# Strided heads of batch 3 brought into the staggered scheme, with their loads moved forward: sparse attention followed by a Mish MLP on one core

## The chip, the cores and the metric

The kernel runs on one core of one Trainium2 chip. The metric is the device time in microseconds of one execution. Before the change it is 306.9 us, the median of three runs (306.23 to 308.34). The profile comes from an execution with a span of 306.6 us on the device, in which TensorE was granted its full clock.

## The reference

Attention over 8 batches, 8 heads, 576 positions and head size 64. Heads 0 to 3 ("local") see the 32 positions up to their own; heads 4 to 7 ("strided") see those earlier positions that are equal to theirs modulo 32. The attention's output, as 4608 tokens by 512, goes through two matrix products with the activation `h * tanh(softplus(h))` (Mish) between them.

```python
scores = scale * np.matmul(q, k.transpose(0, 1, 3, 2))
rel = pos[:, None] - pos[None, :]
mask_local = (rel >= 0) & (rel < stride)                       # stride = 32
mask_strided = (rel >= 0) & (pos[None, :] % stride == pos[:, None] % stride)
masks = np.stack([mask_local if h < H // 2 else mask_strided for h in range(H)], axis=0)
scores = np.where(masks[None, :, :, :], scores, -1000000000.0)
# ... softmax over the last axis ...
attn_out = np.matmul(attn, v)                                  # (8, 8, 576, 64)
x = attn_out.transpose(0, 2, 1, 3).reshape(B * S, H * D)       # (4608, 512)
h = x @ w_in                                                   # (4608, 2048)
sp = np.where(h > 20.0, h, np.log1p(np.exp(np.minimum(h, 20.0))))
out = (h * np.tanh(sp)) @ w_out                                # (4608, 512)
```

## The kernel before

The MLP is done in nine blocks of 512 tokens, t = 0 to 8. In each block `mlp1` is the first product (64 matmuls of 128x128 by 512 columns, then Mish on ScalarE) and `mlp2` the second (also 64). The attention of batch t + 1 is woven into block t, in small pieces between groups of matmuls: list entry i of `at` runs after group i of the second product, entry i of `a1` after group i of the first.

There are two forms for a batch in the middle of the run. In `attn_steps` everything for a batch stands in the second product of one block. In the staggered form, the strided scores of the next batch (kind "n") are made one block ahead, in the second product of the block before; `str_steps` then multiplies them with v in the first product, and `loc_steps` does the local heads in the second. The staggered form also transposes the attention's output on VectorE (`xt_str`, `xt_loc`) instead of TensorE (`xt`).

```python
    def load_qk_str(b):                        # software queue, f32 -> bf16
        for dst, src in ((ks, k), (qs, q)):
            nc.gpsimd.dma_start(dst[b % 2][0:PN], src[b, 4:8].rearrange("h (p j) d -> p h (j d)", j=CS))

    def load_qk_loc(b):                        # SyncE's queue, f32
        for dst, src in ((kl32, k), (ql32, q)):
            nc.sync.dma_start(...)             # [cut]

    # the space of vs32, seen as two bf16 halves
    vsd = vs32[0:PN].rearrange("p h j d -> p (h j d)").bitcast(BF16)
    vsd = [vsd[:, 2048 * i:2048 * i + 2048] for i in range(2)]

    def load_v_str01(b):                       # software queue, f32 -> bf16
        dst = vsd[b % 2].rearrange("p (h x) -> p h x", h=4)
        ...                                    # [cut: batch 0]
            nc.gpsimd.dma_start(dst, v[b, 4:8].rearrange("h (p j) d -> p h (j d)", j=CS))

    def load_v_str(b):                         # SyncE's queue, f32
        nc.sync.dma_start(vs32[0:PN], v[b, 4:8].rearrange("h (p j) d -> p h j d", j=CS))

    def str_by_dma(b):                         # transposed strided k, then q
        for src, dst in ((ks, kTs), (qs, qTs)):
            nc.sync.dma_start_transpose(sT(dst, b)[...], src[b % 2][0:SU]...)   # [cut]

    def str_steps(b):
        a = Attn(b)
        V = lambda i: (lambda: a.pv("s", i))
        return [[], [V(0)], [V(1)], [V(2)], [V(3)], [V(4)], [V(5)], [V(6)], [V(7), a.xt_str]]

    def loc_steps(b, x, y):
        # [cut: Q makes scores and their exponential, M masks on VectorE, V multiplies with v]
        n2 = (("n", 2),) if more else ()
        N = [lambda i=i: a.mask("n", i, nc.gpsimd) for i in range(3)]
        return [
            [],
            [Q(x, ("l", 0)), Q(None, ("l", 2), *n2), Q(y, ("l", 1)), M("l", 0), M("l", 2)],
            [], [],
            [V(0), V(1), M("l", 1)],
            ([Q(x, ("n", 0)), Q(y, ("n", 1))] + N) * more + [a.xt_str_copy, V(5)],
            [V(2)], [V(3)],
            [V(4), lambda: a.xt_loc(0, NW)],
            [], [], [], [], [], [], [],
        ]

    def attn_steps(b, x, y, z=None):           # [cut: its other steps, X transposes on TensorE]
        r = [
            [],
            [Q(x, s0), Q(y, s1), M(*s0), M(*s1)],
            [],
            [V("s", 0), V("s", 1)],
            [Q(x, *sl2), Q(y, l0), V("s", 2)],
            ...
            [X("s", 0), V("l", 2)],
            [X("s", 1), V("l", 3)],
            [V("l", 4), X("l", 0)],
            [X("l", 1)], [],
        ]
        if z is not None:                      # the next batch's strided scores
            r[12].append(Q(x, ("n", 0)))
            r[13].append(Q(z, ("n", 1)))
            r[15] += [Q(x, ("n", 2)), M("n", 0), M("n", 1), M("n", 2)]
        return r
```

Before block 0 the loads of batch 2 are issued, and the loop over blocks issues the later ones:

```python
        load_qk_str(2)
        ...                                    # local q, k of batch 2
        load_v_str01(2)
        load_v_loc_h(2)

        def next_loads():                      # step 1 of block 0's second product
            load_qk_str(3)
            copy_v_str01(2, Po, 0, CS)
            rows_v_loc01(2, 0, 6, Po)

        for t in range(NBLK):
            ...
                if t <= 2:
                    at = attn_steps(t + 1, x, y, z if t == 2 else None)
                elif t + 1 < B:
                    a1 = str_steps(t + 1)
                    at = loc_steps(t + 1, x, y)
                if t == 1:
                    at[9].append(lambda: str_by_dma(3))
                ...
                if t + 2 < B:
                    at[9].append(lambda: loc_by_dma(t + 2))
                if 1 < t < B - 3:
                    at[9].append(lambda: str_by_dma(t + 3))
            ...                                # the first product
            if t > 0 and t + 2 < B:
                cast_qk_loc(t + 2, Po, Po)
                if 1 < t < B - 3:
                    load_qk_str(t + 3)
                if t < 3:
                    cast_v(t + 2, Po, Po)
                else:
                    at[5].append(lambda: cast_v(t + 2, Po, Po))
            if t == 1:
                load_qk_str(4)
            ...                                # the second product
            if t + 3 < B:
                load_qk_loc(t + 3)
                if t == 1:
                    str_by_dma(4)
                load_v(t + 3)
```

Of the kernel before, what the change touches and what calls it, by code (L numbers as in the profile page):

```python
# [40 lines left out]
def kernel(ctx, tc, q, k, v, moe_w_in, moe_w_out, out):  # L41
# [115 lines left out]
    def load_v_str(b):  # L157
        nc.sync.dma_start(vs32[0:PN], v[b, 4:8].rearrange("h (p j) d -> p h j d", j=CS))

    def load_v_loc(b):  # L160
# [2 lines left out]
            vl32[32:128].rearrange("p h w d -> p (h w) d"),  # L163
            v[b, 0:4].rearrange("h (w p) d -> p (h w) d", p=WQ),
        )

    def load_v(b):
        load_v_str(b)
        load_v_loc(b)

    def load_w_in(f0, f1):
        nc.gpsimd.dma_start(  # L172
# [120 lines left out]
    class Attn:  # L293
# [64 lines left out]
        def pv_mm(self, kind, i, po):  # L358
            for h in range(4):
                if kind == "l":  # L360
                    n, rhs = 128, vl[self.b % 2][:, i, h, :]
                    part, u = AT["l"][i, h // 2]
                    pt, c0 = P_l[part][:, h % 2], WQ * u
                else:
                    n, rhs = PN, vs[self.b % 2][0:PN, h, i, :]
                    part, u = AT["n" if self.b > 3 else "s"][i // 2, h]
                    pt, c0 = P_s[part][:, i % 2], PN * u
                nc.tensor.matmul(  # L368
                    po[:, h, :], lhsT=pt[0:n, c0:c0 + 128], rhs=rhs,
                    start=True, stop=True,  # L370
                )
# [250 lines left out]
    with tc.manual_schedule():  # L622
        Po, Dv, Sc = nc.gpsimd, nc.vector, nc.scalar
        Sc.preload_act_table(AF.Exp)
        Sc.dma_start(consts[:], consts_h.ap())
        lq0 = g_pool.tile([128, 16, 512], BF16, tag="gT", name="lq0")
        lq0 = lq0[:].rearrange("p a b -> p (a b)")[0:PL]
        kl0, ql0 = [lq0[:, 1536 * i:1536 * i + 1536].rearrange("p (h x) -> p h x", h=4) for i in range(2)]
        load_str01(ks[0], k, 0)
        load_str01(qs[0], q, 0)  # L630
        load_v_str01(0)
        load_qk_loc01(0, kl0, ql0)
        kl0, ql0 = [x.rearrange("p h (j d) -> p h j d", d=D) for x in (kl0, ql0)]
        Dv.memset(kTs[1][:, 0:640], 0.0)
        Dv.memset(kTs[1][:, 640:], 0.0)
        Dv.memset(vl[0][:, :, :, D:D + 1], 1.0)
        Dv.memset(vl[0][0:32, 0], 0.0)
        load_v_loc01(0, 0, 3)
        load_w_in(0, 256)
        load_v_loc01(0, 3, 6)  # L640
        load_w_in(256, 512)
        load_w_in(512, 1024)
        Dv.memset(vs[0][:, :, :, D:D + 1], 1.0)
        Dv.memset(kTs[0][:, 0:16 * SU].rearrange("p (u n) -> p u n", n=SU)[:, :, PN:], 0.0)
        Dv.memset(kTs[0][:, 16 * SU:], 0.0)
        for p, n in zip(P_s, (6, 6, 4)):
            Dv.memset(p[:, :, n * PN:], 0.0)
        Dv.memset(kTl[:, :, 0:32], 0.0)
        for p, n in zip(P_l, (5, 5, 2)):
            Dv.memset(p[:, :, n * WQ:], 0.0)  # L650
        Dv.memset(vs[1][:, :, :, D:D + 1], 1.0)
        Dv.memset(vl[1][:, :, :, D:D + 1], 1.0)
        Dv.memset(vl[1][0:32, 0], 0.0)
        for x in (ks, qs):
            for h in (0, 2):
                Sc.copy(
                    x[1][64:SU, h:h + 2, :].rearrange("p h x -> p (h x)").bitcast(F32),
                    kTs[1][64:SU, 0:1024].bitcast(F32),
                )

        a = Attn(0)
        fill_acc(2, 11)
        for hp in range(2):
            t_step(0, "k", hp, Sc if hp else Dv)
        a.bias("s", 0, 0)
        fill_acc(2, 4)
        for hp in range(2):
            t_step(0, "q", hp, Sc if hp else Dv)
        a.bias("s", 1, 1)
        fill_acc(2, 1)  # L670
        a.bias("s", 2, 2)
        for i in range(3):
            a.qk([("s", i)], i)
        copy_v_str01(0, Dv, 0, 4)
        copy_v_str01(0, Dv, 4, 8)
        fill(tile_t("fill"), 2)
        a.pv2("s", 0, 0)
        t_step_loc0(kl0, kTl[:, 0, 32:32 + S], 0, Dv)
        t_step_loc0(kl0, kTl[:, 1, 32:32 + S], 1, Sc)
        a.pv2("s", 2, 1)  # L680
        a.pv2("s", 4, 2)
        fill_acc(0, 1)
        t_step_loc0(ql0, qTl[:, 0, :], 0, Sc)
        t_step_loc0(ql0, qTl[:, 1, :], 1, Sc)
        a.pv2("s", 6, 0)
        a.bias("l", 0, 1)
        a.bias("l", 1, 2)
        a.qk([("l", 0)], 1)
        a.qk([("l", 1)], 2)
        rows_v_loc01(0, 0, 3, Po)  # L690
        load_w_in(1024, 1536)
        load_w_in(1536, 2048)
        rows_v_loc01(0, 3, 6, Po)
        load_qk_str(1)
        load_w_out(0, 1)
        load_v_str01(1)
        load_qk_loc01(1, rows(kl[1]), rows(ql[1]))
        load_w_out(1, 3)
        load_v_loc_h(1)
        load_w_out(3, 4)  # L700
        a.bias("l", 2, 0)
        a.qk([("l", 2)], 0)
        a.xt("s", 0, Dv)
        a.xt("s", 1)
        Sc.preload_act_table(AF.Mish)
        a.pv2("l", 0, 1)
        a.pv2("l", 2, 0)
        a.pv2("l", 4, 1)
        accs = (2, 0, 1)
        gT, g1 = mlp1(0, accs)  # L710
        g1.pop(0)()
        a.xt("l", 0)
        g1.pop(0)()
        a.xt("l", 1)
        Dv.memset(vl32[0:32], 0.0)
        for x in (ks, qs):
            Dv.memset(x[0][64:SU], 0.0)
        load_qk_str(2)
        rows_v_loc01(1, 0, 6, Po)
        for dst, src in ((kl, k), (ql, q)):  # L720
            to = by_tile(dst[0])
            for h in range(4):
                nc.gpsimd.dma_start(
                    to[:, h // 2, :, h % 2, :], src[2, h].rearrange("(i p) d -> p i d", p=PL)
                )
        load_v_str01(2)
        load_v_loc_h(2)

        def next_loads():
            load_qk_str(3)  # L730
            copy_v_str01(2, Po, 0, CS)
            rows_v_loc01(2, 0, 6, Po)

        for t in range(NBLK):
            x, y, z = accs
            if t > 0:
                gT, g1 = mlp1(t, accs)
            ts, at, a1 = [], [], []
            if t == 0:
                ts, at = t_steps1(), attn_steps(1, y, y)  # L740
                at[0] += [lambda: Sc.preload_act_table(AF.Exp)]
                at[1] += [lambda: copy_v_str01(1, nc.vector, 0, CS), next_loads]
                at[2] += ts[4:6]
                at[3] += ts[6:8]
                at[9] += [lambda: str_by_dma(2), lambda: loc_by_dma(2)]
                out_accs, accs = (z, x), (y, z, x)
            else:
                if t <= 2:
                    at = attn_steps(t + 1, x, y, z if t == 2 else None)
                elif t + 1 < B:  # L750
                    a1 = str_steps(t + 1)
                    at = loc_steps(t + 1, x, y)
                if t == 1:
                    at[9].append(lambda: str_by_dma(3))
                if t == 2:
                    Dv.memset(x_s[64:96], 0.0)
                if t + 2 < B:
# [3 lines that stand above are left out]
                out_accs, accs = (z, y), (z, x, y)  # L761
            for i, g in enumerate(g1):
                g()
                if i < len(a1):
                    for s in a1[i]:
                        s()
                if t == 0:
                    for n in {6: (0, 1), 7: (2, 3)}.get(i, ()):
                        ts[n]()
            if t > 0 and t + 2 < B:  # L770
                cast_qk_loc(t + 2, Po, Po)
                if 1 < t < B - 3:
                    load_qk_str(t + 3)
                if t < 3:
                    cast_v(t + 2, Po, Po)
                else:
                    at[5].append(lambda: cast_v(t + 2, Po, Po))
            if t == 1:
                load_qk_str(4)
            if t == NBLK - 1:  # L780
                mlp2_last(t, gT, (z, y, x))
                break
            for i, g in enumerate(mlp2(t, gT, out_accs, fc_major=(t == 0))):
                g()
                if i < len(at):
                    for s in at[i]:
                        s()
            if t + 3 < B:
                load_qk_loc(t + 3)
                if t == 1:  # L790
                    str_by_dma(4)
                load_v(t + 3)


# [28 lines left out]
```

## Time and profile before

| | |
|---|---|
| median of 3 runs | 306.9 us |
| span of the profiled execution | 306.6 us |
| VectorE, ScalarE, GpSimd busy | 51%, 60%, 34% of the span |
| TensorE's granted clock | 1.00 |
| mean DMA rate | 136 GB/s |
| read from and written to HBM | 36.82 MB and 9.44 MB |

A row of slices cuts the span into 40 equal parts; a digit is the busy share of one in tenths, 9 being 90% or more. A line of the order in time gives start and length in microseconds, the engine (SPq is SyncE's DMA queue), the line of the kernel, the operation and what it writes and reads; x is the number of instructions merged into it. A queue row gives packets, megabytes and the time its packets took as a share of 16 engines' span.

Names: `psh` is the accumulator of the first product and `pso` that of the second, `ps` holds scores, `po` is attention times v, `trx` the transposes of the attention's output on TensorE. `ks`, `qs`, `vs` are the strided k, q, v; `kl`, `ql`, `vl` the local ones; `kTs`, `qTs`, `kTl`, `qTl` the transposed ones.

### The profile page before, as it was taken

Reading aid. Unit: us, or ns where it says so; the run is one execution under the profiler, and the core shown is the slowest. Engines: PE = TensorE matmul, PEld = TensorE weight load, DVE = VectorE, ACT = ScalarE, POOL = GpSimd, SP = SyncE. Lnnn points to the kernel's source line nnn. Section 1 sums busy time; section 2 is a strip of 40 time slices with the busy share of each in tenths; the row PEclk is TensorE's granted clock in tenths of the full one; section 3 lists DMA queues with packets and bytes.
Section 4 is the critical chain, followed back from the end, with each engine's and each line's share of the span. In section 5 each row is a group of like instructions: output and inputs, shape, how many; then the busy total and the mean of one; then the engine's idle time right before and its main releaser. Section 6 shows DMA issues by size and latency. Waiting matters only on the chain.

```text
span 306.6 us, 5875 instructions
## 1 busy us (share of the span) xinstructions
PE 297.2 (97%) x2431; PEld 154.4 (50%) x2431; DVE 156.8 (51%) x375; ACT 182.9 (60%) x196; POOL 104.0 (34%) x120
## 2 busy tenths in 40 slices
PE   8889999999999999999999999999999999999995
PEld 3544555544554445444578654445444544444444
DVE  3572358201850086579877888787879850000000
ACT  5576553767446763767866786687668746216501
POOL 8592326741246025502980297029600000000000
PEclk9999999999999999999999999999999999999999
DMA  7999999999999999999969996997430120011011
GB/s 112 168 145 201 204 168 145 151 119 186 212 210 134 209 147 209 200 197 193 168 152 179 196 170 147 167 193 125 126 90 0 46 92 0 2 68 68 0 71 68
DMA packets 97558, 41.66 MB, mean 136 GB/s; under 512 B 79612, under 2 KB 91612, under 8 KB 97532
## 3 DMA queue, kind: packets, MB, share of 16 engines
q1 hardware_dynamic: 71564, 28.58, 52.6%
q0 software_dynamic: 25680, 12.46, 35.8%
q8 instruction: 19, 0.31, 0.4%
q10 hardware_dynamic: 288, 0.25, 0.3%
q14 instruction: 7, 0.06, 0.1%
HBM read 36.82 MB, written 9.44 MB: 151 GB/s over the span
## 4 chain that ended last, share of the span: by engine, by line
PE 80%; DMA 11%; DVE 4%; POOL 2%; issue 1%; ACT 0%; POOLq 0%
PE psh L562 36%; PE pso L585 33%; DMA w_out<-in_moe_w_out_dram 5%; PE pso L612 5%; PE po L368 4%; DMA w_in<-in_moe_w_in_dram 3%; DMA lq<-in_q_dram 3%; PE ps L330 3%; DVE x_s L380 1%; DVE Pl L352 1%; DVE x_l L380 1%; DVE rden L379 1%; PE trx L407 1%; POOL w_in L172 0%; POOL ks L110 0%
## 5 line engine op out<-in xcount | busy, mean ns | idle before, releaser
L562 PE MATMUL psh<-xT,w_in 128*128 128x512 bf16 (+1 forms) x640 | 130.6, 358 | 1.0 <-ACT xT L185 0.7
L585 PE MATMUL pso<-w_out,gT 128*128 128x512 bf16 x512 | 121.7, 379 | 0.2 <-DMA w_out<-in_moe_w_out_dram 0.2
L568 ACT ACTIVATE gT<-psh 128x1024 bf16<-128x1024 f32 x72 | 72.4, 1023 | 47.7 <-PE psh L562 47.7
L562 PEld LDWEIGHTS <-w_in 128*128 128x128 bf16 x640 | 60.1, 98 | 56.6 <-issue 1.4
L585 PEld LDWEIGHTS <-gT 128*128 128x128 bf16 x512 | 45.5, 98 | 46.2 <-issue 0.2
L442 DVE STREAM_TRANSPOSE xs_t<-x_s 32x512 bf16<-32x512 bf16 x48 | 33.7, 702 | 0.9
L592 ACT COPY osb<-pso 128x1024 f32<-128x1024 f32 x16 | 17.6, 1099 | 24.6 <-PE pso L585 14.0
L379 DVE RECIPROCAL rden<-po 72x4 f32<-72x4 f32 (+1 forms) x98 | 17.3, 177 | 28.2 <-PE po L368 27.9
L187 POOL CAST kl<-kl 96x768 bf16<-96x768 f32 x10 | 8.5, 876 | 62.3 <-DMA kl<-in_k_dram 53.0
L352 DVE TENSOR_TENSOR Ps<-Ps,consts_sb 72x864 bf16<-72x864 bf16 (+3 forms) x12 | 8.1, 683 | 38.9 <-ACT Ps L344 38.9
L433 DVE STREAM_TRANSPOSE xT<-x_l 32x384 bf16<-32x384 bf16 x48 | 27.3, 569 | 0.7
L187 DVE COPY osb<-pso 128x512 f32<-128x512 f32 (+1 forms) x2 | 1.1, 558 | 51.3 <-PE pso L612 51.3
L380 DVE TENSOR_TENSOR x_s<-po,rden 72x256 bf16<-72x256 f32 x56 | 23.6, 421 | 1.9
L344 ACT ACTIVATE Ps<-ps 72x864 bf16<-72x864 f32 (+3 forms) x21 | 17.4, 860 | 10.7 <-PE ps L330 10.6
L449 ACT COPY xT<-xs_t 128x576 bf16<-128x576 bf16 x8 | 21.4, 2938 | 0.0
L368 PEld LDWEIGHTS <-Ps 72*128 72x128 bf16 x256 | 14.9, 98 | 11.5 <-DVE Ps L352 0.8
L344 ACT ACTIVATE Pl<-ps 128x960 bf16<-128x960 f32 (+1 forms) x20 | 17.1, 875 | 3.7 <-PE ps L330 3.6
L380 DVE TENSOR_TENSOR x_l<-po,rden 96x256 bf16<-96x256 f32 x42 | 17.7, 421 | 1.4
L185 ACT COPY xT<-trx 128x576 bf16<-128x576 bf16 x15 | 9.5, 640 | 14.3 <-PE trx L417 11.7
L368 PE MATMUL po<-vs,Ps 72*128 72x65 bf16 x256 | 17.3, 194 | 0.1
L187 POOL CAST vl<-vl 128x768 bf16<-128x768 f32 (+2 forms) x20 | 15.4, 770 | 4.9 <-DMA vl<-in_v_dram 4.0
L352 POOL TENSOR_TENSOR Ps<-Ps,consts_sb 72x1008 bf16<-72x1008 bf16 (+1 forms) x9 | 14.5, 1650 | 0.1
(90 smaller groups left out, 236.0 us busy)
## 6 DMA issues: line engine op xcount, KB each, us to landing
out_dram<-osb SPq DMA_DIRECT2D x16, 512.0 KB, 4.2
kl<-in_k_dram SPq DMA_DIRECT2D x5, 576.0 KB, 6.9
ql<-in_q_dram SPq DMA_DIRECT2D x5, 576.0 KB, 9.9
vs<-in_v_dram SPq DMA_DIRECT2D x5, 576.0 KB
vl<-in_v_dram SPq DMA_DIRECT2D x5, 576.0 KB, 9.7
w_out<-in_moe_w_out_dram POOLq DMA_DIRECT2D x4, 512.0 KB, 15.9
ks<-in_k_dram POOLq DMA_DIRECT2D x7, 288.0 KB, 9.5
qs<-in_q_dram POOLq DMA_DIRECT2D x7, 288.0 KB, 9.3
```

What stands on the lines that cost most here:

```text
L187: eng.tensor_copy(out_, in_)
L344: nc.scalar.activation(pt[0:n, :, 0:nw], t[0:n, :, o0:o0 + nw], AF.Exp, scale=scale)
L352: meng.tensor_tensor(out=pm, in0=pm, in1=mk[0:n, :].unsqueeze(1).unsqueeze(1).to_broadcast([n, 2, nu, w]), op=ALU.mult,)
L368: nc.tensor.matmul(po[:, h, :], lhsT=pt[0:n, c0:c0 + 128], rhs=rhs, start=True, stop=True,)
L379: nc.vector.reciprocal(rden[0:m, :], po[0:m, :, D])
L380: nc.vector.tensor_tensor(out=dst.rearrange("p (h d) -> p h d", h=4), in0=po[0:m, :, 0:D], in1=rden[0:m, :].unsqueeze(2).to_broadcast([m, ...
L433: nc.vector.transpose(dst[32 * q:32 * q + 32, :, :, m:m + 32], src[m:m + 32, :, :, q, :])
L442: nc.vector.transpose(xs_t[32 * q:32 * q + 32, :, :, m:m + 32], src[m:m + 32, :, :, q, :])
L449: nc.scalar.copy(xT[:, 2 + c, t0:t0 + S].rearrange("p (n j) -> p j n", j=CS), xs_t[:, :, c, 0:PN])
L562: nc.tensor.matmul(ps[:, u, o:o + n], lhsT=w_in[:, cc, fc * 128:(fc + 1) * 128], rhs=xT[:, cc, a:a + n], start=(cc == 2 and o == 0), stop= ...
L568: nc.scalar.activation(gT[:, 2 * g:2 * g + 2, :], ps[:], AF.Mish)
L585: nc.tensor.matmul(p[:, ot % 2, :], lhsT=gT[:, fc, 128 * ot:128 * ot + 128], rhs=w_out[:, fc, :], start=(fc == 0), stop=(fc == 15),)
```

## The change

The staggered form begins at batch 3 instead of batch 4. Block 1 now also makes batch 3's strided scores (kind "n") at the end of its second product, and block 2 runs `str_steps(3)` in its first product and `loc_steps(3)` in its second. So batch 4's strided scores also move from the end of block 2's second product to its steps 1 and 5. The aim is to end the crowding of attention work in block 2's second product and to take the transposes of batch 3's output off TensorE.

For this, data must come earlier. Batch 3's strided q and k are loaded ahead of batch 2's v on the software queue, and transposed at the end of block 0 instead of in block 1. Batch 3's strided v comes as bf16 by the software queue, is copied by GpSimd at the start of block 1, and no longer comes as f32 on SyncE's queue.

```diff
-    def load_v(b):
-        load_v_str(b)
-        load_v_loc(b)
...
-                    part, u = AT["n" if self.b > 3 else "s"][i // 2, h]
+                    part, u = AT["n" if self.b > 2 else "s"][i // 2, h]
...
-        load_v_str01(2)
-        load_v_loc_h(2)
-
         def next_loads():
             load_qk_str(3)
+            load_v_str01(2)
+            load_v_loc_h(2)
+            load_v_str01(3)
             copy_v_str01(2, Po, 0, CS)
             rows_v_loc01(2, 0, 6, Po)
...
-                if t <= 2:
-                    at = attn_steps(t + 1, x, y, z if t == 2 else None)
+                if t == 1:
+                    at = attn_steps(t + 1, x, y, z)
                 elif t + 1 < B:
                     a1 = str_steps(t + 1)
                     at = loc_steps(t + 1, x, y)
-                if t == 1:
-                    at[9].append(lambda: str_by_dma(3))
...
             if t > 0 and t + 2 < B:
+                if t == 1:
+                    copy_v_str01(3, Po, 0, CS)
                 cast_qk_loc(t + 2, Po, Po)
                 if 1 < t < B - 3:
                     load_qk_str(t + 3)
-                if t < 3:
-                    cast_v(t + 2, Po, Po)
+                if t == 1:
+                    cast_v_loc(3, Po)
                 else:
                     at[5].append(lambda: cast_v(t + 2, Po, Po))
...
             if t + 3 < B:
                 load_qk_loc(t + 3)
-                if t == 1:
-                    str_by_dma(4)
-                load_v(t + 3)
+                if t < 2:
+                    str_by_dma(t + 3)
+                if t > 0:
+                    load_v_str(t + 3)
+                load_v_loc(t + 3)
```

## The prediction

> **What bounds the kernel now.** I read the shares of busy time first, then the DMA rows of the slices, then the order in time on TensorE and on the SyncE queue in blocks 0 to 3, and the landings of single transfers.
>
> ```profile
> PE 297.2 (97%) x2431; PEld 154.4 (50%) x2431; DVE 156.8 (51%) x375; ACT 182.9 (60%) x196; POOL 104.0 (34%) x120
> DMA  7999999999999999999969996997430120011011
> q1 hardware_dynamic: 71564, 28.58, 52.6%
> q0 software_dynamic: 25680, 12.46, 35.8%
> ```
>
> TensorE is busy almost throughout, so only TensorE work removed, or TensorE waits, move the time. But the DMA engines are full for the first two thirds of the span, so a deadline moved forward there can turn into such a wait. TensorE's order in time, with the lines that mark the blocks:
>
> ```profile
> 58.03 13.98 PE L562 MATMUL psh<-xT,w_in 128*128 128x512 bf16 x64
> 71.84 1.89 PE L585 MATMUL pso<-w_out,gT 128*128 128x512 bf16 x8
> ...
> 90.51 13.98 PE L562 MATMUL psh<-xT,w_in 128*128 128x512 bf16 x64
> 104.32 1.89 PE L585 MATMUL pso<-w_out,gT 128*128 128x512 bf16 x8
> ...
> 120.31 0.40 PE L330 MATMUL ps<-qTs,kTs 64*128 64x72 bf16 x14
> ...
> 124.59 1.04 PE L562 MATMUL psh<-xT,w_in 128*128 128x512 bf16 x4
> ...
> 139.84 1.89 PE L585 MATMUL pso<-w_out,gT 128*128 128x512 bf16 x8
> 141.67 0.47 PE L330 MATMUL ps<-qTl,kTl 64*128 64x96 bf16 x14
> 141.97 0.23 PE L330 MATMUL ps<-qTs,kTs 64*128 64x72 bf16 x4
> ```
>
> From one start of a first product to the next: block 1 takes 90.51 - 58.03 = 32.48, block 2 34.08, block 3 (124.59 to 155.88) 31.29; block 5, a staggered one without split columns, 30.86 (187.05 to 217.91 in the chain). The line at 120.31 is the first use of batch 4's transposed strided q and k. Now the SyncE queue:
>
> ```profile
> 70.02 8.47 SPq L116 DMA_DIRECT2D ql<-in_q_dram  x1
> 78.60 4.17 SPq L158 DMA_DIRECT2D vs<-in_v_dram  x1
> 82.81 0.66 SPq L162 DMA_DIRECT2D vl<-in_v_dram  x1
> ...
> 102.13 5.08 SPq L116 DMA_DIRECT2D ql<-in_q_dram  x1
> 107.31 5.35 SPq L205 DMA_TRANSPOSE kTs<-ks  x1
> 112.76 2.82 SPq L205 DMA_TRANSPOSE qTs<-qs  x1
> ```
>
> Batch 3's ql landed 16.8 us after its issue, at 86.8; batch 4's ql 13.2 after, at 115.3; then batch 4's kTs (9.1 after) at 116.4 and qTs (4.8 after) at 117.6. So the transposes came through right behind the ql load, 2.3 us later, though their source ks had landed at 101.7 (96.08 + 5.6): the queue's own order held them. Needed at 120.31, they had 2.7 us to spare. In the time slices around there the DMA rate falls to 0 to 10 GB/s from 113.8 to 115.1 and then stands at about 290 for 1.9 us[...].
>
> [...] from 66 to 74 us, with the software queue active (0.62 MB), the hardware queue moves 0.40 MB; from 74 to 82, with the software queue all but empty, 1.91 MB. [...]
>
> **The change, part by part.**
> (1) TensorE work removed. Batch 3 was the last done by attn_steps; now it is done by str_steps and loc_steps, whose transposes run on VectorE. That takes away 16 + 12 = 28 transposes (trx) on TensorE, four groups of 0.42 us as shown in the order in time (their overlap with neighbours leaves some 1.3), and the crowding of block 2's second product. Measured by blocks: block 1 takes the form of old block 2 (34.08, for 32.48), block 2 that of old block 3 (31.29, for 34.08), block 3 that of block 5 (30.86, for 31.29). Sum before 97.85, after 96.23: 1.6 us gained if nothing waits. Masks and transposes move to GpSimd and VectorE, which are 34% and 51% busy and carry exactly this load in blocks 4 and 5 without holding TensorE. The memset of x_s is as before.
> (2) Batch 3's strided q, k. The first use was at the strided scores of block 2, 1.8 us into its second product (106.14). It moves to step 12 of block 1: as in old block 2, 120.31 - 104.32 = 16.0 us into the second product, so 71.84 + 16.0 = 87.8. The transposes stand right behind kl and ql of batch 3 on SyncE. That ql landed at 86.8. The one added competitor is batch 3's strided v on the software queue, whose last landing was 75.5 (63.91 + 11.6): a 288 KB load there costs some 3 us of the engines (the qs of batch 4 landed at 105.0, 3.3 after ks). So ql lands at about 89.8 and qTs at 89.8 + 2.3 = 92.1: TensorE, which takes its matmuls in order, waits 92.1 - 87.8 = 4.3 us.
> (3) Batch 4's strided q, k. They were needed at 120.31 and are now needed at step 1 of block 2's second product: old block 3 has it 141.97 - 124.59 = 17.4 us after the start of its first product; block 2's start is 58.03 + 34.08 + 4.3 = 96.4, so 113.8. When do they land? Before, at 117.6, at the end of a queue that was full except for spells at 96 to 100 us (99 GB/s) and just before 115. What stands ahead of them changes little: the f32 v of batch 3 goes from SyncE's queue (3.4 us at 170 GB/s), its bf16 form comes to the software queue (3 us). The wait of block 2's ks, qs loads for the cast of batch 3's local v, which now follows two transposes, shifts them from 96 to about 100, over the kl, ql loads of batch 4. I take 117: a second wait of 3.2 us.
> (4) Batch 2's v, now behind 576 KB of strided q, k on the software queue: its strided part landed at 66.4 (55.82 + 10.6) and was copied by 68.4; now it lands some 4 to 6 us later and is copied (1.89 us) by 74.3. Its first use is at 75.95. Close, but I count nothing.
> Sum: -1.6 + 4.3 + 3.2 = +5.9, or 312.8. After block 2 the steady blocks have room (batch 5's kTs landed at 134.1 for a use that now comes at 117 + 31 = 148), so the delay neither grows nor is caught up.
>
> **Rivals.**
> - All arrives in time, and the gain of 1.6 us stays: 305.3. For it: the 1.0 us between the old ql landing and the new deadline, the slack DMA time at 96 to 100 and around 114, and that the strided q, k enter the software queue earlier. Against: the transposes come no sooner than ql, and more, not less, is moved ahead of it.
> - Only one of the two waits: 1.6 gained, 3 to 4.5 lost: 308.5 to 310.
> - Batch 2's v comes late (part 4): TensorE would wait at step 3 of block 1, some 75.95, up to 2 us. It would shift the next deadline as well, so it is largely swallowed by the waits after it.
> - An engine becomes the bound: VectorE has 24.4 us of work in old block 3's 30.5 and takes that form one block earlier. Blocks 4 and 5 say no.
>
> **Range and chances.** The second deadline decides: what TensorE can't do before batch 4's qTs is there, it can't do whatever happened at the first. If that comes at 113, the change is worth about +2; at 117.6, +6.5; at 120, +9. Two queues sharing the engines make its time uncertain by 3 us, and the rival without waits has perhaps one chance in four. So I set 311.0, between the sum and that rival, 304.9 to 316.5. Over 2% faster would need 300.8, which no part offers: 0.02. Over 2% slower begins at 313.0, near my sum: 0.34.
>
> **What would show it.** Right: TensorE idle before strided scores near 88 to 92 us and again near 114 to 117, released by qTs; trx matmuls down by 28; ql of batch 3 landing near 89 to 90. Wrong: the first strided scores of batch 3 at 87.8 without a gap, and block 3's first product at or before 123.4 (124.59 less 1.2). If transposes were found to pass the loads ahead of them, part 2 and 3 fall, and the time is 305.

## Result, and the profile after

The changed kernel takes 310.04 us (median of 4, 309.51 to 310.70) against 306.63: a ratio of 1.0102, interval 1.0055 to 1.0148. Run again beside two of the later experiments, it took 312.86 us (median of 6, 310.66 to 313.88) against 306.82: 1.0179, interval 1.0140 to 1.0218. It is slower, by 1 to 2%. The ratios leave out executions more than 1.5% above the same kernel's fastest; as the waits found here lengthen executions by about that much, the median of all executions is given beside each ratio.

From the page of the changed kernel: shares of busy time, the rows of slices for the granted clock and the DMA, and the two queues.

```profile
PE 294.2 (95%) x2365; PEld 154.0 (50%) x2403; DVE 172.7 (56%) x396; ACT 185.6 (60%) x196; POOL 110.9 (36%) x124
PEclk9999999999999979999999999999999999999999
DMA  7999999999999998489978996998430020011011
q1 hardware_dynamic: 71264, 27.99, 48.6%
q0 software_dynamic: 26080, 12.76, 34.0%
```

TensorE has less work (28 weight loads fewer, PEld), VectorE more, as meant, and the software queue carries 0.3 MB more. The trace lacks 38 matmul records, so x63, x7 and x11 below stand for 64, 8 and 12. New is the 7 in the row of the clock, in the slice from 108 to 116 us. TensorE's order in time, the lines that answer to those of before (start, length, line, operation, and in brackets idle time with what ended it):

```profile
56.98 13.98 PE L558 MATMUL psh<-xT,w_in 128*128 128x512 bf16 x63
70.79 1.89 PE L581 MATMUL pso<-w_out,gT 128*128 128x512 bf16 x7
...
82.44 0.29 PE L364 MATMUL po<-vl,Pl 128*128 128x65 bf16 x4 [0.94 <-PE po L364]
...
87.60 0.40 PE L326 MATMUL ps<-qTs,kTs 64*128 64x72 bf16 x14
...
91.89 1.04 PE L558 MATMUL psh<-xT,w_in 128*128 128x512 bf16 x4
...
107.13 1.89 PE L581 MATMUL pso<-w_out,gT 128*128 128x512 bf16 x8
108.95 0.47 PE L326 MATMUL ps<-qTl,kTl 64*128 64x96 bf16 x14
111.98 0.30 PE L326 MATMUL ps<-qTs,kTs 64*128 64x72 bf16 x4 [2.56 <-DMA qTs<-qs]
112.07 0.62 PE L326 MATMUL ps<-qTl,kTl 64*128 64x96 bf16 x10
113.02 3.57 PE L581 MATMUL pso<-w_out,gT 128*128 128x512 bf16 x11 [0.33 <-issue]
...
127.36 1.89 PE L558 MATMUL psh<-xT,w_in 128*128 128x512 bf16 x8
```

Read by blocks, from one first product's start to the next:

| | before | after | predicted if nothing waits |
|---|---|---|---|
| block 1 | 32.48 | 34.91 | 34.08 |
| block 2 | 34.08 | 35.47 | 31.29 |
| block 3 | 31.29 | 30.85 | 30.86 |
| sum | 97.85 | 101.23 | 96.23 |

The sum grows by 3.38 us, as the medians do (3.41). (The profiled execution happened to enter block 1 1.05 us earlier, so its span grew by only 2.3.) The 1.62 gained is there, and 5.0 are lost: 0.83 in block 1, 4.18 in block 2. Of those 4.18, 2.56 are the wait for batch 4's qTs in the line at 111.98, in which TensorE ran none of the matmuls that stand behind it (nothing from 109.42 to 111.98). The rest stands in the product's next twelve matmuls, which take 3.57 us. Before the change, at the same step, then in block 3, they took 2.76:

```profile
142.35 2.76 PE L585 MATMUL pso<-w_out,gT 128*128 128x512 bf16 x12
```

Stretches of 1 us around the wait, with TensorE's busy time and instructions, granted clock, DMA share and GB/s, show why:

```profile
110.00:111.00 1.00, 0.00 (x0) 1.00 0.98 167
111.00:112.00 1.00, 0.02 (x2) 0.84 0.70 71
112.00:113.00 1.00, 0.69 (x14) 0.50 0.43 106
113.00:114.00 1.00, 0.98 (x3) 0.50 0.98 284
114.00:115.00 1.00, 1.00 (x4) 0.50 0.97 180
115.00:116.00 1.00, 1.00 (x6) 0.95 1.23 189
```

After the wait the clock is halved until shortly after 115. From 111.98, at half clock, some 3.1 us of work are worth 1.55: the remainder. Not every execution pays it: of the four in the first comparison, two had a granted clock of 0.994 (310.53 and 310.70 us) and two of 1.00 (309.51 and 309.56).

The SyncE queue of the changed kernel at the same place:

```profile
95.50 0.47 SPq L116 DMA_DIRECT2D kl<-in_k_dram  x1
96.02 5.20 SPq L116 DMA_DIRECT2D ql<-in_q_dram  x1
101.32 6.59 SPq L201 DMA_TRANSPOSE kTs<-ks  x1
108.01 1.36 SPq L201 DMA_TRANSPOSE qTs<-qs  x1
```

Batch 4's ql landed at 108.9 (12.9 after issue), its kTs at 110.0 (8.7) and qTs at 111.9 (3.9). Again the transposes follow the ql load.

Block 1's 0.83 shows on VectorE and GpSimd. First the mask of the strided scores before, on VectorE; then the same mask after, with GpSimd's line beside it:

```profile
79.58 0.45 DVE L352 TENSOR_TENSOR Ps<-Ps,consts_sb 72x576 bf16<-72x576 bf16 x1
```

```profile
78.53 1.80 DVE L348 TENSOR_TENSOR Ps<-Ps,consts_sb 72x576 bf16<-72x576 bf16 x1
```

```profile
78.14 1.89 POOL L183 COPY vs<-vs 72x2048 bf16<-72x2048 bf16 x1 [1.06 <-DMA vs<-in_v_dram]
```

The mask starts while GpSimd copies batch 3's strided v (this copy stands between block 1's two products, not at the block's start) and ends 0.3 us after that copy. The masks and divisions behind it on VectorE come later too, up to 82.34, and TensorE waits 0.94 us, until 82.44; the list of before has no wait over 0.25 us in this block. The releaser named there is an earlier matmul, so that the mask is behind this wait is argued here and tested below. What in the copy makes the mask longer, 1.80 us against 0.45, is not shown.

### The profile page after: what moved, and what is told of

Read it like the earlier page. It is cut to its first block, busy times and chain, and to the rows that moved or that the text cites. A ratio compares the mean times of both kernels' runs of the same rounds, so it can differ in the third digit from the quotient of the medians.

```text
span 308.9 us, 5806 instructions
## 1 busy us (share of the span) xinstructions
PE 294.2 (95%) x2365; PEld 154.0 (50%) x2403; DVE 172.7 (56%) x396; ACT 185.6 (60%) x196; POOL 110.9 (36%) x124
## 4 chain that ended last, share of the span: by engine, by line
PE 75%; SPq 10%; DMA 5%; DVE 3%; ACT 2%; POOL 2%; issue 2%; POOLq 0%; ACTq 0%
PE psh L558 33%; PE pso L581 29%; SPq L116 5%; SPq L201 5%; PE pso L608 4%; PE po L364 4%; PE ps L326 2%; DMA vl<-in_v_dram 2%; DMA qs<-in_q_dram 2%; DMA qTs<-qs 1%; POOL vl L183 1%; DVE x_s L376 1%; ACT Pl L340 1%; DVE x_s L390 1%; ACT Ps L340 1%
## 5 line engine op out<-in xcount | busy, mean ns | idle before, releaser
L581 PE MATMUL pso<-w_out,gT 128*128 128x512 bf16 x487 | 118.0, 382 | 2.1 <-issue 1.0
L581 PEld LDWEIGHTS <-gT 128*128 128x128 bf16 x512 | 46.2, 98 | 48.6 <-issue 1.6
L438 DVE STREAM_TRANSPOSE xs_t<-x_s 32x512 bf16<-32x512 bf16 x60 | 42.1, 702 | 1.2
L429 DVE STREAM_TRANSPOSE xT<-x_l 32x384 bf16<-32x384 bf16 x60 | 34.1, 569 | 0.9
L445 ACT COPY xT<-xs_t 128x576 bf16<-128x576 bf16 x10 | 26.8, 2940 | 0.0
L340 ACT ACTIVATE Ps<-ps 72x1008 bf16<-72x1008 f32 (+3 forms) x20 | 17.0, 883 | 12.9 <-PE ps L326 12.9
L348 POOL TENSOR_TENSOR Ps<-Ps,consts_sb 72x1008 bf16<-72x1008 bf16 (+1 forms) x12 | 19.4, 1644 | 7.2 <-DVE x_l L376 7.2
L364 PE MATMUL po<-vl,Pl 128*128 128x65 bf16 x192 | 12.5, 195 | 2.0 <-PE po L364 0.9
```

What stands on the lines that cost most here:

```text
L340: nc.scalar.activation(pt[0:n, :, 0:nw], t[0:n, :, o0:o0 + nw], AF.Exp, scale=scale)
L348: meng.tensor_tensor(out=pm, in0=pm, in1=mk[0:n, :].unsqueeze(1).unsqueeze(1).to_broadcast([n, 2, nu, w]), op=ALU.mult,)
L364: nc.tensor.matmul(po[:, h, :], lhsT=pt[0:n, c0:c0 + 128], rhs=rhs, start=True, stop=True,)
L429: nc.vector.transpose(dst[32 * q:32 * q + 32, :, :, m:m + 32], src[m:m + 32, :, :, q, :])
L438: nc.vector.transpose(xs_t[32 * q:32 * q + 32, :, :, m:m + 32], src[m:m + 32, :, :, q, :])
L445: nc.scalar.copy(xT[:, 2 + c, t0:t0 + S].rearrange("p (n j) -> p j n", j=CS), xs_t[:, :, c, 0:PN])
```

## Experiments

Three questions. Do the transposes come late because of their place in SyncE's queue (theory Q), because the engines are full whatever the order (rival E), or because their source ks, qs is late (rival S)? Does the wait also cost clock (theory C)? Is block 1's loss GpSimd's copy (theory G)?

**Order for batch 4 only.** The transposes of batch 4 ahead of its kl, ql loads; those of batch 3 as in the change.

```diff
+                if t == 1:
+                    str_by_dma(t + 3)
                 load_qk_loc(t + 3)
-                if t < 2:
+                if t == 0:
                     str_by_dma(t + 3)
```

> Theory Q (queue order): batch 4's transposed strided q, k come late because they stand behind the kl, ql loads of batch 4 on SyncE's queue. Put ahead of those loads, they wait for ks, qs alone (landed at about 101 and 106 in the changed kernel), so qTs lands before about 109 and TensorE's 2.6 us wait in block 2 goes, with the 1.6 us of half clock after it: 310.0 becomes 305.5 to 307. Rival E (the engines are simply full): the bytes that have to move first are the same, qTs still lands at 111 to 112, and the time stays at 309.5 to 310.5. The kl, ql loads come some 8 us later in either case; if that matters, a new wait shows in block 3.

Median of 11 executions 310.27 us, but from 305.78 to 312.33; ratio 1.0027 (0.9985 to 1.0069). The wait of block 2 is gone from the profiled execution, but TensorE waits in block 1 instead, for batch 3's transposes, which still stand behind their ql:

```profile
90.15 0.40 PE L326 MATMUL ps<-qTs,kTs 64*128 64x72 bf16 x14 [2.98 <-DMA qTs<-qs]
...
113.36 0.23 PE L326 MATMUL ps<-qTs,kTs 64*128 64x72 bf16 x4
```

Part of this is that the use itself came later. Counted from the start of block 2, though, qTs landed after 14.9 us (110.92 - 95.98) and in the change after 20.1 (111.94 - 91.89), while TensorE wants it after 17.4 to 17.5. Q holds for batch 4, and the expected time came in the best executions only: the first deadline is just as real, though it was met in the first profile of the change. The change's second profile, from the repeated run, shows both waits:

```profile
88.01 0.41 PE L326 MATMUL ps<-qTs,kTs 64*128 64x72 bf16 x14 [1.81 <-DMA qTs<-qs]
...
113.54 0.24 PE L326 MATMUL ps<-qTs,kTs 64*128 64x72 bf16 x4 [2.15 <-DMA qTs<-qs]
```

> The changed kernel once more, on the same chip and beside the same runs of the kernel before. The theories differ only over the others; here 309 to 311.5 is expected, with a spread of some 3 us, as in every variant that left the wait for the transposes of batch 4 in place, and a granted clock of 0.994 or below in the executions in which the wait halves the clock.

All six executions had a clock of 0.995 or less. Four of the six, and the median of 312.86, lie above what I expected.

**Load of ks, qs of batch 4 early only.**

```diff
                 cast_qk_loc(t + 2, Po, Po)
+                if t == 1:
+                    load_qk_str(4)
...
-            if t == 1:
-                load_qk_str(4)
```

> Batch 4's ks, qs are loaded before GpSimd's cast of batch 3's local v instead of after it; the order on SyncE stays. Theory Q: qTs still waits for the ql load ahead of it, and comes earlier only by what the ks, qs loads no longer take from kl, ql, some 1 to 2 us: 308 to 309.5. Rival S (the source ks, qs sets the transposes' time): they move up by the 5 to 8 us by which the loads do, the wait goes, and the time is 305.5 to 307.

ks and qs were issued at 86.8 and 87.5 and landed by 97.6, but the transposes came after ql (landed at 109.6), qTs at 111.7; a wait of 1.16 us was left. Median 311.85 us, ratio 1.0206 (1.0150 to 1.0263): not faster, and above what Q expected as well. S falls: the source was there 14 us before qTs, and qTs still came some 2 us after ql.

**Matmuls in place of the wait.**

```diff
                     at = loc_steps(t + 1, x, y)
+                    if t == 2:
+                        at[1].insert(1, lambda: fill_w(12))   # 12 matmuls of 512 columns, unread
```

> Twelve matmuls of 512 columns (2.6 us) whose result nobody reads stand just ahead of the late strided scores in block 2, so that TensorE works where it waited. Theory C (the wait also costs clock): the granted clock stays at 1.00, the twelve matmuls after it run at 0.22 us each, and the time is 308.5 to 309.3, below 310.0, although work was added. Rival: the slow stretch after the wait has another cause (the DMA, the pipeline), and the time stays at 310 or rises.

Here qTs came only at 114.0, so 2.00 us of wait were left after the twelve. Still the clock stayed at 1.00 in the profiled execution, and from the release to block 3 it took 127.95 - 114.03 = 13.9 us, the same as before the change (155.88 - 141.97 = 13.9), against 127.36 - 111.98 = 15.4 in the change. So the 1.5 us after the wait are the clock's. The time did not fall: median 313.33 us of 4, ratio 1.0124 (1.0081 to 1.0167). In the total my expectation failed, as a late qTs moves the end whatever TensorE does meanwhile. The clock failed it as well: in two of the four executions it was 0.989.

**GpSimd's copy of v later,** behind its casts of kl and ql.

```diff
-                if t == 1:
-                    copy_v_str01(3, Po, 0, CS)
                 cast_qk_loc(t + 2, Po, Po)
+                if t == 1:
+                    copy_v_str01(3, Po, 0, CS)
```

> GpSimd's copy of batch 3's strided v stands behind its casts of kl, ql instead of ahead of them. Theory G: that copy (78.1 to 80.0) slowed VectorE's mask (1.80 us instead of 0.45) and so block 1 by 0.8 us; the mask goes back to below 1.1 us, block 1's second product takes 20.3 instead of 21.1. If the wait in block 2 has a fixed end set by the DMA, the time stays near 309.5 to 310 all the same; if it moves along, it is 309.2. Rival: the mask is as slow as before, and block 1 is unchanged.

The mask took 0.80 us. Block 1 lasted 35.80 us with a wait of 1.91 for qTs in it, so 33.9 without: the 0.83 is gone, G holds. But the two waits for qTs were 1.91 and 4.91 us, and the median is 312.76 us (ratio 1.0208, 1.0172 to 1.0244): all gained there is waited for later, and more; the time is above the 309.2 to 310 expected. Why qTs came so late for block 2 is not shown.

**Both orders.**

```diff
-                load_qk_loc(t + 3)
                 if t < 2:
                     str_by_dma(t + 3)
+                load_qk_loc(t + 3)
```

> Theory Q, for both deadlines: the transposes of batch 3's and of batch 4's strided q, k each stand ahead of the kl, ql loads of the same batch on SyncE. Neither wait is left: block 1 as before plus at most 0.8 us of the slowed mask, block 2's second product 16.0 us, granted clock 1.00 throughout. 304.8 to 306.2, below the kernel before by 0.5 to 1.6 us. Rival E (engines full): one of the waits comes back elsewhere, at the local scores of block 2 or 3, whose kl, ql now come 4 to 8 us later, and the time stays above 307.

In the profiled execution neither wait is left, and block 2 takes 31.28 us (91.29 to 122.57), predicted 31.29:

```profile
87.00 0.40 PE L326 MATMUL ps<-qTs,kTs 64*128 64x72 bf16 x14
...
108.67 0.23 PE L326 MATMUL ps<-qTs,kTs 64*128 64x72 bf16 x4
```

It took 306.55 us, but it is the fastest of 14 executions. Eight stayed above 309, the median is 310.19, the ratio 1.0048 (1.0014 to 1.0082). That is outside what I expected of Q: the waits can be removed by the order, but in many executions something else was late, or the same transposes again, and this profile does not show which.

**Both orders and the copy later.**

> As the run with both orders changed, and GpSimd's copy of batch 3's strided v behind its casts. With the waits gone, the slowed mask is on the path: theory G expects 0.5 to 0.8 us less than the run with both orders alone, 304.3 to 305.5. Rival: the casts of kl, ql, which now come later, slow some other mask as much, and it is the same within 0.3 us.

Median 309.97 us of 22, ratio 1.0060 (1.0037 to 1.0083): G's gain did not come. The profiled execution, at 314.26 us the slowest of the 22, shows two new waits:

```profile
84.59 0.29 PE L364 MATMUL po<-vl,Pl 128*128 128x65 bf16 x4 [1.55 <-POOL vl L183]
...
99.23 0.28 PE L364 MATMUL po<-vs,Ps 72*128 72x65 bf16 x4 [2.88 <-POOL vs L183]
```

The second is my own making: kl and ql now come later, and the copy waited behind their casts. The first is batch 2's local v, which the change put behind the strided q, k.

**Without the load of batch 3's strided v.** Leaves out `load_v_str01(3)`, so batch 3's strided heads use older data.

```diff
-            load_v_str01(3)
```

> The changed kernel without the software load of batch 3's strided v (so batch 3's strided heads are computed from older data, and the output differs there); everything else stays. By step 2 of the prediction the load costs kl, ql of batch 3 some 3 us: ql lands 13 to 14 us after its issue instead of 16.0, and no wait is left at the first strided scores of batch 3 in any execution; the later wait shrinks too, 308 to 309.5. Rival: the load runs beside the others in time that the engines had anyway, ql lands 15.5 to 16.5 us after its issue, and the time stays at 309.5 to 310.5.

ql of batch 3 landed 14.4 us after its issue (16.0 and 17.5 in the two profiles of the change), no wait in block 1, one of 2.07 us in block 2. So the load delays the queue, by 1.6 to 3.1 us in these executions; the one profiled, at 307.40 us, is the fastest of its twenty. Yet the time is 310.58 us (median of 20; ratio 1.0092, 1.0072 to 1.0112), like the change. This load is not what makes it slow.

**Batch 2's v first,** as it was before the change.

```diff
         def next_loads():
-            load_qk_str(3)
             load_v_str01(2)
             load_v_loc_h(2)
+            load_qk_str(3)
             load_v_str01(3)
```

> The changed kernel with the old order on the software queue: batch 2's v ahead of batch 3's strided q, k. Theory Q: the transposes of batch 3 wait for ql ahead of them, not for ks, qs, so the order on the software queue does nothing for them: 309.5 to 310.7, with batch 2's strided v landing some 4 us earlier. Rival S (the source sets the time): ks, qs land some 4 us later than before, at 68 to 75, and if the transposes follow them, TensorE waits at the first strided scores of batch 3 for 2 us or more: 312 or above.

GpSimd could copy batch 2's strided and local v at 63.7 and 68.0 instead of 67.9 and 75.8. ks and qs of batch 3 landed at 70.2 and 73.7, well ahead of ql at 84.8, so again they set nothing; the waits were 1.43 and 3.51 us. Median 311.91 us, ratio 1.0145 (1.0086 to 1.0204), which overlaps that of the change: no clear effect of its own. The median is above the 309.5 to 310.7 expected of Q.

**Both orders, batch 2's v first; and with batch 4's ks, qs early as well.** The two versions combine edits shown above.

> Both transposes ahead of the kl, ql loads, and batch 2's v back ahead of batch 3's strided q, k on the software queue. Theory Q with V (the executions of the run with both orders alone that stayed slow waited for batch 2's local v, which lands late behind the strided q, k): neither the strided scores nor the local v of batch 2 wait; 305.0 to 306.3, executions within 2 us of each other. Rival E (engines full): some other transfer is late in turn, and many executions stay at 309 to 312.

> As the run before it, and batch 4's ks, qs loaded ahead of GpSimd's cast of batch 3's local v. In the run with both orders alone batch 4's qTs landed at 107.8 for a use at 108.7; here it lands some 4 us earlier, so a late execution does not wait: 305.0 to 306.0. Rival: the software load then delays the local transposes and v of batch 3, and it is 0.5 us or more slower than without.

The first: median 308.78 us of 14, ratio 1.0047 (1.0021 to 1.0072), with seven above 309. That misses the expectation: batch 2's local v was there in time (landed by 74.1), so its lateness alone does not explain the slow executions. ks and qs of batch 4 landed late in the profiled one (issued at 98.6 and 99.3), and qTs with them, a wait of 2.32. Now, with ql out of the way, the source does set the time: SyncE issued the two transposes at 104.62 and 107.17, as ks and qs landed at 104.60 and 107.15. The second: median 306.42 us of 14 (304.91 to 309.10), a little above the 305.0 to 306.0 expected, ratio 0.9986 (0.9958 to 1.0014), no execution with a lowered clock. In the wait list of its profile no DMA holds TensorE from block 1's scores to block 2's; what is left there:

```profile
PE psh L558 <- ACT Ps L340: 0.3, 1, 0.3
PE pso L581 <- PE ps L326: 0.2, 1, 0.2
PE pso L581 <- issue: 0.2, 1, 0.2
```

Beside it the change itself took 312.86: the order in the queues is worth 6.4 us, 2%. As the same data are moved, full engines alone (rival E) do not explain the loss. Both orders with the early load, but without batch 2's v first, were not tried, so whether all three are needed is open. Blocks 1 to 3 of this version take 35.15, 31.28 and 30.85 us: sum 97.28, 0.57 below before. Blocks 2 and 3 are as predicted without waits; block 1 is 1.07 longer, with a mask of 2.12 us beside GpSimd's copy.

**The same with the copy on ScalarE.**

```diff
                     at = attn_steps(t + 1, x, y, z)
+                    at[8].append(lambda: copy_v_str01(3, Sc, 0, CS))
...
-                if t == 1:
-                    copy_v_str01(3, Po, 0, CS)
```

> The last version (both transposes ahead of kl, ql; batch 2's v first on the software queue; batch 4's ks, qs early), with the copy of batch 3's strided v on ScalarE, which stands idle for some 4 us at step 8 of block 1's second product, instead of on GpSimd beside VectorE's mask. Theory G: no mask of block 1 takes more than 1.1 us, its second product takes 20.3 instead of 20.8 to 21.1, and the time falls by 0.4 to 0.8 us to 305.6 to 306.0, below the kernel before. Rival: GpSimd's casts of kl slow the next mask as much, or ScalarE's copy holds up the copies of xT, and it is 306.4 or above.

Median 307.42 us of 23 (304.99 to 313.72), ratio 0.9999 (0.9979 to 1.0019). The mask that had taken 1.80 us is at 0.45 and none takes over 0.68, as G has it, but the expected gain is not measured. The profiled execution, at 313.72 us the slowest of the 23, lost 5.48 us to another transfer, the transposed local q of batch 2:

```profile
81.38 0.67 PE L326 MATMUL ps<-qTl,kTl 64*128 64x96 bf16 x12 [5.48 <-DMA qTl<-ql]
```

So E may keep a part: a transfer can come late in this order too. Why this one did is not shown. None of these versions is clearly faster than the kernel before.

## Why the prediction was right, and where not

The time lies in the range (304.9 to 316.5) and near the 311.0 given; direction and mechanism held. The sum of +5.9 was too high against 3.4 of the first comparison and about right for the 6.0 of the second (312.86 - 306.82). That it comes so near is in part luck: the two waits, put at 7.5 us together, were 2.56 and 3.96 in the two profiles, and losses that the sum did not have made up for some of it. The 6.0 is not taken apart by any profile, as the execution profiled there took 310.81 us.

- **Part 1, -1.6 us:** right as far as it goes. trx fell from 112 to 84, and blocks 2 and 3 took 31.28 and 30.85 where nothing waited (31.29 and 30.86 predicted); block 1 did not keep to its 34.08, because of the mask below.
- **Part 2, a first wait of 4.3 us:** mechanism right, size too large. It was 0 in one profile of the change and 1.81 in the other. The mis-sized term is the landing of batch 3's ql, put at 89.8; it landed at 84.0 and 85.0, as SyncE reached it 2 us sooner and nothing was added to its 16.8 us (16.0 and 17.5). My 3 us for the extra load were 1.6 to 3.1, but the old 16.8 to which I added them did not hold for the new order.
- **Part 3, a second wait of 3.2 us:** right in place and cause, 2.56 and 2.15 in size. Arrival (117) and use (113.8) were both set late: 111.9 and 109.4. Batch 4's ks and qs, put at about 100, were issued at 94.7 and 95.5.
- **Missing from the sum:** the half clock after a wait, 1.6 us in the first profile, and the mask beside the moved copy (1.80 us against 0.45), 0.8. I had written that masks move without holding TensorE; I looked at busy shares, not at which instructions would overlap. With that copy moved, block 1 took 33.9 us without its wait.
- **Part 4, batch 2's v:** its strided part came in time, as counted (landed at 67.9, 1.4 us later than before instead of 4 to 6). That its local part could be late I did not see; it cost 1.55 us in one profile.
- **The rival "all arrives in time"** came true only after three reorderings, and then with 0.4 us of gain instead of 1.6, which is within the noise.

Rival S was true only behind Q: each cause hid the next. What stays open is what makes single transfers land several us later from one execution to another: the kernel before, too, spread over some 3.7 us beside the versions with three orders (305.96 to 309.63), and one of its 51 executions beside earlier ones took 311.06 us at a clock of 0.994. In its profile the transposes of batch 4 had 2.8 us of room (117.5 for 120.31).

## What to carry to other kernels

When work is moved a stage earlier, list for each operand its landing and its new deadline, and look at what stands ahead of it in its own queue: here a small urgent transfer behind a large one that nobody needed yet arrived just after the large one (qTs at 111.9 us in the change, ql ahead of it at 108.9). Take a DMA margin of one profile for a sample: the same transposes were in time in one profile of the change and 1.81 us late in the other. And see which instruction a moved copy will run beside (here a mask that took 1.80 us instead of 0.45).

## What the runs showed of the hardware

The clock did not follow the length of the wait. In the change it was halved from 111.7 to 115.1 us after 2.56 us of idle, and in its second profile from 89.1 to 92.5 after only 1.81: for 3.4 us both times. In the run with batch 2's v first a wait of 3.51 us (109.78 to 113.29) lowered nothing:

```profile
110.00:111.00 1.00, 0.00 (x0) 1.00 1.05 225
111.00:112.00 1.00, 0.00 (x0) 1.00 0.99 176
112.00:113.00 1.00, 0.00 (x0) 1.00 0.81 126
113.00:114.00 1.00, 0.55 (x15) 1.00 0.37 88
114.00:115.00 1.00, 1.00 (x6) 1.00 0.89 262
```

The longest waits of other profiles from block 1 on, beside the mean clock of the same execution:

| run | longest wait, us | mean clock |
|---|---|---|
| load of ks, qs early only | 1.16 | 0.999 |
| matmuls in place of the wait | 2.00 | 1.00 |
| without batch 3's strided v | 2.07 | 1.00 |
| both orders, batch 2's v first | 2.32 | 0.994 |
| both orders and the copy later | 2.88 | 0.993 |
| order for batch 4 only | 2.98 | 0.994 |
| copy of v later | 4.91 | 0.989 |
| the last version, copy on ScalarE | 5.48 | 0.989 |

In these the clock was lower where the wait was longer than 2.07 us; the 1.81 and the 3.51 us above do not fit that. What decides it is not shown.
